# Attention on transposed scores without the row maximum, behind a test of the gains, with TensorE in program order

## The chip, the cores and the metric

The kernel runs on one core of a Trainium2 chip. The metric is the device time of one execution in microseconds (us), lower is better. A core has five engines that run beside each other and wait for each other by semaphores: TensorE (PE: products and transposes; PEld: its weight loads), VectorE (DVE), ScalarE (ACT), GpSimd (POOL) and SyncE (SP, which issues the DMAs here). [...]

## The reference

Everything is fp32, but the weights w_in and w_out arrive as doubles and are rounded in the kernel. Cut to what matters:

```python
batch, n_heads, seq, head_dim = (8, 12, 448, 64)
q_n, k_n = (rmsnorm(q, g_q), rmsnorm(k, g_k))
scores = q_n @ k_n.T / sqrt(64)
attn = exp(scores - max(scores, axis=-1))
attn = attn / (sum(attn, axis=-1) + 1e-09)
x = (attn @ v)                      # to (3584, 768)
h = maximum(x @ w_in, 0)            # w_in 768 x 2048
out = (h * h) @ w_out               # w_out 2048 x 768
```

rmsnorm divides a row of 64 by its root mean square and multiplies it by the gains g.

## The kernel before

Attention runs on one pair of heads at a time: 2 x 64 makes 128 partitions, 6 pairs in a batch, 48 in all. The 448 tokens of a sequence are split as token = 4 p + j, with p on 112 partitions.

For a pair i, `load` brings q, k and v (SP). `norm` makes the normalised rows qkn on POOL (squares, a sum on DVE, a power, two products with the factors). `transposes` turns them in eight PE transposes into the PSUM tile pt, and DVE writes them with the gains as qkT, with the head's 64 elements on the partitions.

A unit of work is one j of the queries of one pair, four a pair. `softmax(i, j)` makes the scores sc of 112 queries by 448 keys, for the two heads; DVE takes the maximum of each row (nmax), ACT makes the exponentials pr and their sums, DVE the reciprocal and the scaling of pr. `values(i, j)` transposes pr with eight PE transposes (ppt), copies them out (prT; ACT and DVE one head each), and multiplies them with v into pav, four products a head. After the fourth unit pav goes to xT, which is x transposed.

`feed_forward(b)` is a generator: 16 pieces of the first product ph (six products of 448 columns, then ACT's relu, then POOL's square into gT), then pieces of the second product po (of 384 columns; 16 accumulate one half of 128 tokens; six such halves in an even batch, eight in an odd one). The main loop lays the feed-forward pieces of batch b - 1 between the units of batch b; batch 0 has none, and in it the weights are loaded and rounded instead (`round_weights`: DVE, ACT and POOL, 32 pieces). The feed-forward block of batch 7 runs alone at the end.

The order on each engine is decided by the framework's scheduler, from its own estimate of when an instruction could start; the program's order is its starting point. Tiles come from pools with a number of buffers (`bufs`), and a buffer's next use waits until its readers are done. [...]

Of the kernel before, what the change touches and what calls it, by code (L numbers as in the profile page):

```python
# [1 line left out]

# [6 lines left out]
F32 = mybir.dt.float32  # L9
U32 = mybir.dt.uint32  # L10
AF = mybir.ActivationFunctionType
ALU = mybir.AluOpType
AX = mybir.AxisListType.X


@with_exitstack
def kernel(
    ctx: ExitStack,
    tc: tile.TileContext,
    q: bass.AP,  # L20
# [5 lines left out]
    w_out: bass.AP,  # L26
    out: bass.AP,
):
    """Softmax attention with RMS-normalised q and k, then relu(x w_in)^2 w_out, all in fp32.

    Attention runs on one pair of heads at a time (2 x 64 = 128 partitions).
    A sequence of 448 tokens is split as token = 4 p + j, with p on 112
    partitions, so that a partition's 4 tokens are one run in memory. A unit of
    work is one j of the queries of one pair: scores and softmax with the
    queries on the partitions, then the normalised rows are transposed and
    multiplied with v, which gives x transposed, as the first product of the
    feed-forward block takes it. The feed-forward block of a batch is laid
    between the units of the next batch.
    """
    nc = tc.nc  # L40

    B, H, S, D = q.shape
    NT, DM = out.shape
    DFF = w_in.shape[1]
    P = 128
    NJ = 4
    SP = S // NJ
    NPAIR = H // 2
    NFC = DFF // P
    HALF = DM // 2  # L50
    REST = S % P
    FULL = S - REST
# [3 lines left out]
    consts = ctx.enter_context(tc.tile_pool(name="consts", bufs=1))  # L56
    loads = ctx.enter_context(tc.tile_pool(name="loads", bufs=2))
    work = ctx.enter_context(tc.tile_pool(name="work", bufs=2))
    small = ctx.enter_context(tc.tile_pool(name="small", bufs=4))
    ps_s = ctx.enter_context(tc.tile_pool(name="ps_s", bufs=2, space=bass.MemoryType.PSUM))  # L60
    ps_o = ctx.enter_context(tc.tile_pool(name="ps_o", bufs=1, space=bass.MemoryType.PSUM))
    ps_m = ctx.enter_context(tc.tile_pool(name="ps_m", bufs=3, space=bass.MemoryType.PSUM))

    ident = consts.tile([P, P], F32, name="ident")
    gains = consts.tile([P, 2], F32, name="gains")
    mhalf = consts.tile([SP, 2 * 2 * NJ], F32, name="mhalf")
    w1 = consts.tile([P, NPAIR, DFF], F32, name="w1")
    w2 = consts.tile([P, NFC, DM], F32, name="w2")
    gT = consts.tile([P, NFC, S + REST], F32, name="gT")
    rebias = consts.tile([P, 1], F32, name="rebias")  # L70

# [1 line left out]
    # Doubles come in pairs of words (low, high) and are rounded here to fp32, the  # L73
    # widest type of the engines: +-2^E from the high word, times
    # 1 + (m20 + low 2^-32) 2^-20. Below fp32's normal range a weight becomes 0,
    # above it infinite. The words stay in gT until the feed-forward block needs it.
    NW = 768
    NSET = 3
    spare = gT.rearrange("p f n -> p (f n)")
    assert NSET * 3 * NW <= NFC * (S + REST)  # L80
    doubles = w_in.dtype != F32
    words_in = 2 if doubles else 1
    w1r, w2r = ((w.bitcast(U32) if doubles else w).rearrange("(c p) n -> p c n", p=P) for w in (w_in, w_out))
    CW = NPAIR // 2
    FW = NW // CW
    pieces_w = [(w1[:, c:c + CW, f:f + FW], w1r[:, c:c + CW, words_in * f:words_in * (f + FW)])
                for f in range(0, DFF, FW) for c in (0, CW)]
# [28 lines left out]
        nc.vector.scalar_tensor_tensor(wu, high, 0x80000000, wu, ALU.bitwise_and, ALU.bitwise_or)  # L116
        nc.gpsimd.tensor_tensor(w, f, w, ALU.mult)  # L117

# [1 line left out]
    qks, vs, qkTs, probs, pavs, xTs = {}, {}, {}, {}, {}, {}  # L120

    def load(i):
        b, h0 = i // NPAIR, 2 * (i % NPAIR)
        qk = loads.tile([SP, 2, 2, NJ * D], F32, tag="qk", name="qk")
        vt = loads.tile([SP, 2, NJ, D], F32, tag="vt", name="vt", bufs=3)
        for dst, src in ((qk[:, 0], q), (qk[:, 1], k), (vt.rearrange("p h j d -> p h (j d)"), v)):
            nc.sync.dma_start(dst, src[b, h0:h0 + 2].rearrange("h (p j) d -> p h (j d)", j=NJ))
        qks[i], vs[i] = qk, vt

    normed = {}  # L130
# [20 lines left out]
    def transposes(i):  # L151
        qkn = normed.pop(i)
        qkT = work.tile([P, 2, S], F32, tag="qkT", name="qkT")
        for s in range(2):
            pt = ps_m.tile([P, S], F32, tag="m", name="pt")
            for j in range(NJ):
                nc.tensor.transpose(pt[:, j * SP:(j + 1) * SP],
                                    qkn[:, s, j].rearrange("p h d -> p (h d)"), ident[:SP, :SP])
            nc.vector.tensor_scalar(qkT[:, s], pt, gains[:, s:s + 1], None, ALU.mult)  # L159
        qkTs[i] = qkT  # L160
# [49 lines left out]
                                  pav.rearrange("d (j p) -> d j p", j=NJ))  # L210
            del pavs[i], vs[i]

# [1 line left out]
    # gT has room for 448 + 64 tokens. An even batch takes the last 448 columns  # L214
    # and leaves its last 64 tokens there for the odd batch that follows, which
    # takes the first 448 and shares its last block of 128 with them.
    def feed_forward(b):
        xT = xTs.pop(b)
        odd = b % 2
        c0 = 0 if odd else REST  # L220
        for f in range(NFC):
            ph = ps_m.tile([P, S], F32, tag="m", name="ph")
            for c in range(NPAIR):
                nc.tensor.matmul(ph, w1[:, c, f * P:(f + 1) * P], xT[:, c, :],  # L224
                                 start=(c == 0), stop=(c == NPAIR - 1))
            r = work.tile([P, S], F32, tag="r", name="r")
            nc.scalar.activation(r, ph, AF.Relu)  # L227
            nc.gpsimd.tensor_tensor(gT[:, f, c0:c0 + S], r, r, ALU.mult)  # L228
            yield
        for t in range(0, FULL + P * odd, P):  # L230
            osb = work.tile([P, DM], F32, tag="osb", name="osb")
            for half in range(2):
                cols = slice(half * HALF, (half + 1) * HALF)
                po = ps_m.tile([P, HALF], F32, tag="m", name="po")
                for f in range(NFC):
                    nc.tensor.matmul(po, gT[:, f, c0 + t:c0 + t + P], w2[:, f, cols],  # L236
                                     start=(f == 0), stop=(f == NFC - 1))
                    if f == NFC // 2 - 1:
                        yield
                if half == 0:  # L240
                    nc.vector.tensor_copy(osb[:, cols], po)  # L241
                else:
                    nc.scalar.copy(osb[:, cols], po)
                if half == 1:
                    if t < FULL:
                        nc.sync.dma_start(out[b * S + t:b * S + t + P, :], osb)
                    else:
                        nc.sync.dma_start(out[b * S + FULL:(b + 1) * S, :], osb[0:REST])
                        nc.sync.dma_start(out[(b - 1) * S + FULL:b * S, :], osb[REST:P])
                yield  # L250

    def pieces(b):
        return NFC + 4 * (FULL // P + b % 2)

# [1 line left out]
    load(0)  # L256
    for i, g in enumerate((g_q, g_k)):
        for h in range(2):
# [11 lines left out]
    NP = B * NPAIR  # L270
    last = None
    for b in range(B):
        fill = feed_forward(b - 1) if b else iter(())  # starts at its first next()
        n = pieces(b - 1) if b else 0
        done = 0
        for u in range(NPAIR * NJ):
            i, j = b * NPAIR + u // NJ, u % NJ
            if j == 0 and i + 2 < NP:
                load(i + 2)
            softmax(i, j)  # L280
            if j == 1 and i + 1 < NP:
                norm(i + 1)
            if j == 3 and i + 1 < NP:
                transposes(i + 1)
            if last is not None:
                values(*last)
            last = (i, j)
            if b == 0:
                m = len(pieces_w)
                for n_w in range(m * u // (NPAIR * NJ), m * (u + 1) // (NPAIR * NJ)):  # L290
                    round_weights(n_w)
                    load_weights(n_w + NSET)
            while done < n * (u + 1) // (NPAIR * NJ):
                next(fill)
                done += 1
        for _ in fill:
            pass
# [2 lines left out]
        pass  # L300


# [1 line left out]
_INS = ['q', 'k', 'v', 'g_q', 'g_k', 'moe_w_in', 'moe_w_out']  # L304
_OUTS = [((3584, 768), 'float32')]
# [25 lines left out]
```

## Time and profile before

| | us |
|---|---|
| median of three runs | 2096.86 (2093.71 to 2096.97) |
| the profiled execution | 2093.7 |
| its span, first to last instruction | 2093.7 |
| PE busy | 1981.1 |
| DVE busy | 838.1 |
| POOL busy | 535.5 |
| ACT busy | 494.4 |

PE's busy time counts the records of products, which overlap and whose ends are modelled: the distance between starts tells more of what a product costs. [...] Names such as ph<-xT,w say which tile is written from which; L224 is line 224 of the kernel before.

### The profile page before, as it was taken

Reading aid. Unit: us, or ns where it says so; the run is one execution under the profiler, and the core shown is the slowest. Engines: PE = TensorE matmul, PEld = TensorE weight load, DVE = VectorE, ACT = ScalarE, POOL = GpSimd, SP = SyncE. Lnnn points to the kernel's source line nnn. Section 1 sums busy time; section 2 is a strip of 40 time slices with the busy share of each in tenths; the row PEclk is TensorE's granted clock in tenths of the full one; section 3 lists DMA queues with packets and bytes.
Section 4 is the critical chain, followed back from the end, with each engine's and each line's share of the span. In section 5 each row is a group of like instructions: output and inputs, shape, how many; then the busy total and the mean of one; then the engine's idle time right before and its main releaser. Section 6 shows DMA issues by size and latency. Waiting matters only on the chain.

```text
span 2093.7 us, 22618 instructions
## 1 busy us (share of the span) xinstructions
PE 1981.1 (95%) x9088; PEld 1130.0 (54%) x9088; DVE 838.1 (40%) x1533; ACT 494.4 (24%) x1181; POOL 535.5 (26%) x408
## 2 busy tenths in 40 slices
PE   4767699999999999999999999999999999999999
PEld 2444455555555555555555555555555555555555
DVE  7898853333333333333333333333333333333000
ACT  2344332212221222212221122212222122221100
POOL 4345542311321132311231123221231113210100
PEclk7566599999999999999999999999999999999999
DMA  4233300000000010010000000001000000000000
GB/s 149 93 128 104 123 27 13 28 29 21 23 18 21 29 31 17 14 35 29 14 23 26 29 21 27 14 21 42 14 14 33 31 21 15 17 8 16 0 8 23
DMA packets 47784, 70.67 MB, mean 34 GB/s; under 512 B 3648, under 2 KB 35904, under 8 KB 47680
## 3 DMA queue, kind: packets, MB, share of 16 engines
q1 hardware_dynamic: 47680, 69.22, 10.2%
q8 instruction: 73, 1.20, 0.2%
q14 instruction: 31, 0.25, 0.0%
HBM read 58.20 MB, written 11.01 MB: 33 GB/s over the span
## 4 chain that ended last, share of the span: by engine, by line
PE 81%; DVE 13%; issue 5%; POOL 1%; DMA 0%; SPq 0%; ACT 0%; POOLq 0%; DVEq 0%; ACTq 0%
PE ph L224 29%; PE po L236 25%; PE pav L204 12%; PE sc L167 8%; PE ppt L195 7%; DVE nmax L170 3%; DVE pr L180 1%; DVE qkT L159 1%; DVE w L116 1%; DVE gT L113 1%; DVE gT L112 1%; DVE w L110 1%; DVE rstd L140 1%; DVE w L115 1%; POOL qkn L137 1%
## 5 line engine op out<-in xcount | busy, mean ns | idle before, releaser
L224 PE MATMUL ph<-xT,w 128*128 128x448 f32 x1536 | 626.8, 549 | 1.1 <-DVE xT L209 1.1
L236 PE MATMUL po<-w,gT 128*128 128x384 f32 x1792 | 617.7, 492 | 0.0
L170 DVE TENSOR_REDUCE nmax<-sc 112x2 f32<-112x896 f32 x192 | 209.2, 1090 | 799.2 <-PE sc L167 799.2
L236 PEld LDWEIGHTS po<-w,gT 128*128 128x128 f32 x1792 | 326.7, 190 | 207.8 <-DVE qkT L159 2.8
L224 PEld LDWEIGHTS ph<-xT,w 128*128 128x128 f32 x1536 | 275.0, 190 | 231.2 <-issue 208.0
L204 PEld LDWEIGHTS pav<-prT,vt 112*64 112x64 f32 x3072 | 275.2, 144 | 165.4 <-ACT prT L198 104.3
L204 PE MATMUL pav<-prT,vt 112*64 112x112 f32 x3072 | 334.4, 278 | 6.8 <-DVE prT L200 6.2
L228 POOL TENSOR_TENSOR gT<-r 128x448 f32<-128x448 f32 x128 | 119.4, 933 | 752.7 <-ACT r L227 752.7
L174 ACT ACTIVATE pr<-sc,nmax 112x448 f32<-112x448 f32 x384 | 240.2, 630 | 184.8 <-DVE nmax L170 180.3
L167 PE MATMUL sc<-qkT 64*112 64x448 f32 x768 | 228.9, 626 | 34.0 <-DVE qkT L159 17.5
L195 PE MATMUL ppt<-ident,pr 112*112 112x112 f32 x1536 | 207.8, 277 | 42.6 <-DVE pr L180 23.1
L195 PEld LDWEIGHTS ppt<-ident,pr 112*112 112x112 f32 x1536 | 158.4, 140 | 152.9 <-issue 113.4
L137 POOL TENSOR_TENSOR qkn<-qk 112x1024 f32<-112x1024 f32 x48 | 91.8, 1912 | 533.3 <-issue 380.7
L227 ACT ACTIVATE r<-ph 128x448 f32<-128x448 f32 x128 | 69.6, 544 | 602.5 <-PE ph L224 602.5
L198 ACT COPY prT<-ppt 112x448 f32<-112x448 f32 x192 | 102.1, 532 | 412.6 <-PE ppt L195 412.6
L180 DVE TENSOR_SCALAR pr<-pr,rec 112x448 f32<-112x448 f32 x384 | 174.5, 497 | 5.8
L142 POOL TENSOR_TENSOR rstd<-rstd,mhalf 112x16 f32<-112x16 f32 x48 | 139.6, 2909 | 4.0
L167 PEld LDWEIGHTS sc<-qkT 64*112 64x112 f32 x768 | 61.1, 183 | 147.3 <-issue 105.2
L200 DVE COPY prT<-ppt 112x448 f32<-112x448 f32 x192 | 118.0, 614 | 16.0 <-PE ppt L195 15.9
L144 POOL TENSOR_TENSOR qkn<-qk,rstd 112x512 f32<-112x512 f32 x96 | 107.1, 1136 | 3.8
L241 DVE COPY osb<-po 128x384 f32<-128x384 f32 x28 | 15.6, 558 | 229.0 <-PE po L236 229.0
L117 POOL TENSOR_TENSOR w<-gT,w 128x768 f32<-128x768 f32 x32 | 65.4, 2047 | 112.5 <-DVE w L116 65.3
(27 smaller groups left out, 630.4 us busy)
## 6 DMA issues: line engine op xcount, KB each, us to landing
gT<-in_moe_w_in_dram SPq DMA_DIRECT2D x16, 768.0 KB, 4.5
gT<-in_moe_w_out_dram SPq DMA_DIRECT2D x16, 768.0 KB, 4.2
qk<-in_q_dram SPq DMA_DIRECT2D x48, 224.0 KB, 2.7
qk<-in_k_dram SPq DMA_DIRECT2D x48, 224.0 KB, 2.9
vt<-in_v_dram SPq DMA_DIRECT2D x48, 224.0 KB, 2.5
out_dram<-osb SPq DMA_DIRECT2D x24, 384.0 KB, 2.3
out_dram<-osb SPq DMA_DIRECT2D x8, 192.0 KB, 2.6
gains<-in_g_q_dram SPq DMA_DIRECT2D x2, 0.2 KB, 2.8
```

The costliest lines, as they stand in the source:

```text
L137: nc.gpsimd.tensor_tensor(sq, flat, flat, ALU.mult)
L142: nc.gpsimd.tensor_tensor(rflat, rflat, mhalf, ALU.pow)
L167: nc.tensor.matmul(sc[:, h, 0:S], qkT[rows, 0, j * SP:(j + 1) * SP], qkT[rows, 1, :], start=True, stop=True)
L170: nc.vector.tensor_reduce(nmax, sc[:, :, 0:S], AX, ALU.max, negate=True)
L174: nc.scalar.activation(pr[:, h], sc[:, h, 0:S], AF.Exp, bias=nmax[:, h:h + 1], accum_out=total[:, h:h + 1])
L180: nc.vector.tensor_scalar(pr[:, h], pr[:, h], rec[:, h:h + 1], None, ALU.mult)
L195: nc.tensor.transpose(pt[:, c, :], pr[:, h, c * SP:(c + 1) * SP], ident[:SP, :SP])
L200: nc.vector.tensor_copy(prT, pt)
L204: nc.tensor.matmul(pav[h * D:(h + 1) * D, j * SP:(j + 1) * SP], vt[:, h, c, :], prTs[h][:, c, :], start=(c == 0), stop=(c == NJ - 1))
L224: nc.tensor.matmul(ph, w1[:, c, f * P:(f + 1) * P], xT[:, c, :], start=(c == 0), stop=(c == NPAIR - 1))
L228: nc.gpsimd.tensor_tensor(gT[:, f, c0:c0 + S], r, r, ALU.mult)
L236: nc.tensor.matmul(po, gT[:, f, c0 + t:c0 + t + P], w2[:, f, cols], start=(f == 0), stop=(f == NFC - 1))
```

## The change

The function above stays, as `attention_then_ffn_with_row_max`. Beside it stands a second one, `attention_then_ffn_bounded`, and the kernel chooses between them at run time: it loads the two gains, takes the largest (g_q g_k)^2, and every engine loads that number into a register and branches. If it is at most 75^2 / 64 = 87.9, no score can exceed 75, the exponentials don't need the row maximum, and the bounded function runs. With the reference's gains the number is 27.7.

In the bounded function the scores are made transposed, with the keys on the partitions: `scores(i, c)` has 112 keys by 448 queries for the two heads, and one ACT operation makes the exponentials pr of both. pr is then already the operand that `values` needs, so its transposes and copies are gone; a product is 448 columns wide instead of 112, and the two heads alternate. POOL adds the four pr of a pair into acc, and `finish(i)` multiplies acc with a tile of ones, which gives the sums of the columns (tot) on 64 partitions; DVE takes the reciprocal of 128 x 448 and multiplies pav with it. The loads of v are issued apart from those of q and k. A block of work is now two key chunks, twelve blocks a batch, and feed-forward pieces of po are whole halves. `ps_m` has two buffers, `ps_o` a second tile (tot). The relu writes into gT and POOL squares it there.

The bounded function runs under `manual_schedule` for PE: PE's instructions keep the order in which the program is written. The other engines are still ordered by the scheduler.

```diff
-def tile_qk_norm_attention__then__act_relu_squared_kernel(
+def attention_then_ffn_with_row_max(
...
+    ps_m = ctx.enter_context(tc.tile_pool(name="ps_m", bufs=2, space=bass.MemoryType.PSUM))
...
+    def scores(i, c):
+
+        qkT = qkTs[i]
+        sc = ps_s.tile([SP, 2, 512], F32, tag="s", name="sc")
+        for h in range(2):
+            rows = slice(h * D, (h + 1) * D)
+            nc.tensor.matmul(sc[:, h, 0:S], qkT[rows, 1, c * SP:(c + 1) * SP], qkT[rows, 0, :],
+                             start=True, stop=True)
+        pr = work.tile([SP, 2, S], F32, tag="pr", name="pr", bufs=5)
+        nc.scalar.activation(pr, sc[:, :, 0:S], AF.Exp)
+        probs[i, c] = pr
+        if c == 1:
+            accs[i] = work.tile([SP, 2, S], F32, tag="acc", name="acc")
+            nc.gpsimd.tensor_tensor(accs[i], probs[i, 0], pr, ALU.add)
+        elif c > 1:
+            nc.gpsimd.tensor_tensor(accs[i], accs[i], pr, ALU.add)
+        if c == NJ - 1:
+            del qkTs[i]
+
+    def values(i, cs):
+        if 0 in cs:
+            pavs[i] = ps_o.tile([P, S], F32, tag="o", name="pav")
+        for c in cs:
+            pr = probs.pop((i, c))
+            for h in range(2):
+                nc.tensor.matmul(pavs[i][h * D:(h + 1) * D, :], vs[i][:, h, c, :], pr[:, h, :],
+                                 start=(c == 0), stop=(c == NJ - 1))
+
+    def finish(i):
+        b, hp = divmod(i, NPAIR)
+        acc = accs.pop(i)
+        tot = ps_o.tile([P, S], F32, tag="t", name="tot")
+        for h in range(2):
+            nc.tensor.matmul(tot[h * D:(h + 1) * D, :], ones, acc[:, h, :], start=True, stop=True)
+        rec = work.tile([P, S], F32, tag="rec", name="rec", bufs=1)
+        nc.vector.reciprocal(rec, tot)
...
+        nc.vector.tensor_tensor(xTs[b][:, hp, :].rearrange("d (p j) -> d j p", j=NJ),
+                                pavs.pop(i).rearrange("d (j p) -> d j p", j=NJ),
+                                rec.rearrange("d (j p) -> d j p", j=NJ), ALU.mult)
+        del vs[i]
...
+            if not second:
+                if i + 2 < NP:
+                    load(i + 2)
+                scores(i, 0)
+                scores(i, 1)
+                if i + 1 < NP:
+                    norm(i + 1)
+                if u:
+                    values(i - 1, (2, 3))
+                    finish(i - 1)
+            else:
+                if i + 1 < NP:
+                    load_v(i + 1)
+                    transposes(i + 1)
+                scores(i, 2)
+                scores(i, 3)
+                values(i, (0, 1))
...
+            if u == blocks - 1:
+                values(i, (2, 3))
+                finish(i)
+            while done < n * (u + 1) // blocks:
+                next(fill)
+                done += 1
...
+    for i, g in enumerate((g_q, g_k)):
+        nc.sync.dma_start(gg[:, i, :], g.rearrange("(o d) -> o d", o=1))
+    nc.vector.tensor_tensor(gg[:, 0, :], gg[:, 0, :], gg[:, 1, :], ALU.mult)
+    nc.vector.tensor_tensor(gg[:, 0, :], gg[:, 0, :], gg[:, 0, :], ALU.mult)
+    nc.vector.tensor_reduce(top, gg[:, 0, :], AX, ALU.max)
+
+    bits = nc.values_load(top.bitcast(mybir.dt.int32))
+    limit = struct.unpack("<i", struct.pack("<f", 75.0 ** 2 / D))[0]
+    args = (q, k, v, g_q, g_k, w_in, w_out, out)
+    with tc.If(bits <= limit) as small_scores:
+        with tc.manual_schedule(engines={mybir.EngineType.PE}):
+            attention_then_ffn_bounded(tc, *args)
+    with small_scores.Else():
+        attention_then_ffn_with_row_max(tc, *args)
```

What this makes of PE's order, in a stretch of a batch that has ph pieces between. Before, a unit and a half (L167 the scores, L195 the transposes of pr, L204 the values, L224 the feed-forward; L157 transposes q and k of the next pair):

```order
L224 MATMUL ph<-xT,w_79 128x448 x5
L167 MATMUL sc<-qkT 112x448 x2
L157 MATMUL pt<-ident,qkn 128x112 x8
L195 MATMUL ppt<-ident,pr 112x112 x8
L224 MATMUL ph<-xT,w_79 128x448
L204 MATMUL pav<-prT,vt 64x112 x4
L224 MATMUL ph<-xT,w_79 128x448
L204 MATMUL pav<-prT,vt 64x112 x4
L224 MATMUL ph<-xT,w_79 128x448 x4
L167 MATMUL sc<-qkT 112x448 x2
```

Now, a whole pair of heads (two blocks) and the end of the one before, where the line numbers are those of the changed file (L465 scores, L484 values, L492 the column sums, L513 ph, L454 the transposes of q and k):

```order
L492 MATMUL tot<-acc,ones 64x448 x2
L513 MATMUL ph<-xT,w_100 128x448 x12
L454 MATMUL pt<-ident,qkn 128x112 x8
L465 MATMUL sc<-qkT 112x448 x4
L484 MATMUL pav<-pr,vt 64x448 x4
L513 MATMUL ph<-xT,w_100 128x448 x12
L465 MATMUL sc<-qkT 112x448 x4
L484 MATMUL pav<-pr,vt 64x448 x4
L492 MATMUL tot<-acc,ones 64x448 x2
```

Between the transposes pt and the column sums tot, twelve products of ph stand in this order. In the last block of a batch they don't (L525 is po):

```order
L525 MATMUL po<-w_101,gT 128x384 x32
L454 MATMUL pt<-ident,qkn 128x112 x8
L465 MATMUL sc<-qkT 112x448 x4
L484 MATMUL pav<-pr,vt 64x448 x8
L492 MATMUL tot<-acc,ones 64x448 x2
L525 MATMUL po<-w_101,gT 128x384 x32
```

There tot follows the values at once, and the po pieces come behind it. POOL's order at that place, with the numbers of the tiles: qkn_1488 is the norm of the pair after next (its first row waits for pt of the pair before it), acc_1335 the sum that the tot above reads.

```order
L472 TENSOR_TENSOR acc_1335<-pr_1328,pr_1333 112x896
L434 TENSOR_TENSOR qkn_1488<-qk_1322 112x1024
L438 TENSOR_SCALAR rstd_1490<-rstd_1490 112x16
L439 TENSOR_TENSOR rstd_1490<-rstd_1490,mhalf_99 112x16
L441 TENSOR_TENSOR qkn_1488<-qk_1322,rstd_1490 112x2x4x64
L474 TENSOR_TENSOR acc_1335<-acc_1335,pr_1411 112x896
L441 TENSOR_TENSOR qkn_1488<-qk_1322,rstd_1490 112x2x4x64
L474 TENSOR_TENSOR acc_1335<-acc_1335,pr_1417 112x896
```

The norm's first four rows stand ahead of both last additions to acc, its fifth between them. From batch 1 on the same rows stand in this order in every pair of heads.

## Rows read from the trace of the kernel before

**Rows 1.** The page: PE's busy time, and the chain by engine.

```profile
PE 1981.1 (95%) x9088; PEld 1130.0 (54%) x9088; DVE 838.1 (40%) x1533; ACT 494.4 (24%) x1181; POOL 535.5 (26%) x408
...
PE 81%; DVE 13%; issue 5%; POOL 1%; DMA 0%; SPq 0%; ACT 0%; POOLq 0%; DVEq 0%; ACTq 0%
```

**Rows 2.** Busy us by stage: length, PE, PEld, DVE, ACT, POOL; clock, DMA share, GB/s.

```profile
0.00:265.00 265.00, 177.05 (x716) 110.11 (x717) 225.47 (x324) 97.65 (x182) 124.78 (x74) 0.64 0.36 118
265.00:1935.00 1670.00, 1650.28 (x7929) 935.53 (x7928) 609.79 (x1206) 386.12 (x980) 395.76 (x318) 1.00 0.07 23
1935.00:2093.70 158.70, 153.80 (x446) 84.36 (x444) 2.86 (x5) 10.62 (x20) 14.91 (x16) 1.00 0.03 10
```

**Rows 3.** PE's order in time, mid-run: start, length, operation, count, wait.

```profile
1021.68 1.01 PE L167 MATMUL sc<-qkT 64*112 64x448 f32 x4
1022.62 0.98 PE L195 MATMUL ppt<-ident,pr 112*112 112x112 f32 x8
1023.44 0.93 PE L224 MATMUL ph<-xT,w 128*128 128x448 f32 x2
1024.30 1.42 PE L204 MATMUL pav<-prT,vt 112*64 112x112 f32 x16
1025.65 8.54 PE L224 MATMUL ph<-xT,w 128*128 128x448 f32 x22
1034.12 1.01 PE L167 MATMUL sc<-qkT 64*112 64x448 f32 x4
...
1044.83 0.59 PE L195 MATMUL ppt<-ident,pr 112*112 112x112 f32 x4 [0.49 <-DVE qkT L159]
```

**Rows 4.** The same view, a stretch with the second product.

```profile
1182.23 9.94 PE L236 MATMUL po<-w,gT 128*128 128x384 f32 x30
1192.10 1.01 PE L167 MATMUL sc<-qkT 64*112 64x448 f32 x4
```

**Rows 5.** Groups by line, POOL and DVE: busy us, mean ns, idle before.

```profile
L142 POOL TENSOR_TENSOR rstd<-rstd,mhalf 112x16 f32<-112x16 f32 x48 | 139.6, 2909 | 4.0
L228 POOL TENSOR_TENSOR gT<-r 128x448 f32<-128x448 f32 x128 | 119.4, 933 | 752.7 <-ACT r L227 752.7
...
L144 POOL TENSOR_TENSOR qkn<-qk,rstd 112x512 f32<-112x512 f32 x96 | 107.1, 1136 | 3.8
...
L137 POOL TENSOR_TENSOR qkn<-qk 112x1024 f32<-112x1024 f32 x48 | 91.8, 1912 | 533.3 <-issue 380.7 <-PE pt L157 141.5 <-DVE rec L178 3.3
...
L140 DVE TENSOR_REDUCE rstd<-qkn 112x16 f32<-112x1024 f32 x48 | 58.5, 1218 | 27.0 <-POOL qkn L137 27.0
```

**Rows 6.** End of batch 0: PE's order, and two stretches as in rows 2.

```profile
257.61 0.96 PE L195 MATMUL ppt<-ident,pr 112*112 112x112 f32 x4 [3.99 <-DVE pr L180]
...
235.00:262.00 27.00, 15.27 (x78) 10.88 (x77) 27.00 (x40) 11.97 (x23) 17.76 (x9) 0.64 0.38 131
262.00:300.00 38.00, 36.37 (x178) 19.95 (x178) 23.69 (x42) 12.15 (x27) 19.45 (x14) 0.99 0.06 19
```

**Rows 7.** Two small operations of DVE: shortest, median and longest in ns.

```profile
L177 DVE TENSOR_SCALAR total<-total x192: 146/165/1852, 23.3 to 1921.4; 112x2 f32<-112x2 f32 x192
...
L178 DVE RECIPROCAL rec<-total x192: 148/166/167, 23.8 to 1921.6; 112x2 f32<-112x2 f32 x192
```

**Rows 8.** Groups by line, DVE: busy us, mean ns, idle before.

```profile
L170 DVE TENSOR_REDUCE nmax<-sc 112x2 f32<-112x896 f32 x192 | 209.2, 1090 | 799.2 <-PE sc L167 799.2
...
L180 DVE TENSOR_SCALAR pr<-pr,rec 112x448 f32<-112x448 f32 x384 | 174.5, 497 | 5.8
...
L200 DVE COPY prT<-ppt 112x448 f32<-112x448 f32 x192 | 118.0, 614 | 16.0 <-PE ppt L195 15.9
...
L209 DVE COPY xT<-pav 128x448 f32<-128x448 f32 x48 | 46.0, 959 | 73.3 <-PE pav L204 73.3
```

**Rows 9.** The start: a load of gains (KB, us to landing), PE's first work.

```profile
gains<-in_g_q_dram SPq DMA_DIRECT2D x2, 0.2 KB, 2.8
...
12.03 2.01 PE L157 MATMUL pt<-ident,qkn 112*128 112x112 f32 x8 [12.03 <-POOL qkn L144]
```

More of the change, by code (lines that the diff above doesn't have):

```diff
@@ L1 @@
+import struct
 from contextlib import ExitStack
@@ L16 @@
 @with_exitstack
-def kernel(
+def attention_then_ffn_with_row_max(
     ctx: ExitStack,
@@ new lines, with kernel @@
+@with_exitstack
+def kernel(
+    ctx: ExitStack,
+    tc: tile.TileContext,
+    q: bass.AP,
+    k: bass.AP,
+    v: bass.AP,
+    g_q: bass.AP,
+    g_k: bass.AP,
+    w_in: bass.AP,
+    w_out: bass.AP,
+    out: bass.AP,
+):
+    nc = tc.nc
+    D = q.shape[-1]
+    bound = ctx.enter_context(tc.tile_pool(name="bound", bufs=1))
+    gg = bound.tile([1, 2, D], F32, name="gg")
+    top = bound.tile([1, 1], F32, name="top")
+    for i, g in enumerate((g_q, g_k)):
+        nc.sync.dma_start(gg[:, i, :], g.rearrange("(o d) -> o d", o=1))
[10 more added lines that the diff above has]
+        attention_then_ffn_with_row_max(tc, *args)
```

187 lines of the change are left out of this document (added).

## The prediction

> **What bounds the kernel now.** I read the page first, then the busy time by stages, then PE's order in time. PE is busy for 95% of the span, and the chain that ended last is PE for 81% [rows 1], so PE's own work is the thing to cost. The stages differ, though [rows 2]. Batch 0 (to 265 us, where the first feed-forward product starts) has no feed-forward work to fill PE: DVE is busy for 225.5 of 265 us there, PE has waits and a mean granted clock of 0.64. From 265 to 1935 us PE is busy for 1650 of 1670 us at clock 1.00: seven batches of attention, with the feed-forward block of the batch before laid between. The last 158.7 us are the feed-forward block of batch 7 alone.
>
> In the middle stage I price PE by the distance between starts, since the ends are modelled [rows 3]. An fp32 product is two records (passes). Twenty-two passes of ph take 1034.12 - 1025.65 = 8.47 us, 0.385 us each with the change of shape at both ends; thirty passes of po take 9.87 us, 0.329 each [rows 4]. The stage holds 7 x 16 x 6 = 672 products of ph (1344 passes) and 4 x 96 + 3 x 128 = 768 of po (1536 passes): 517.4 + 505.3 = 1022.7 us, which the change leaves alone. What is left, 1670 - 1022.7 = 647 us over 42 pairs of heads, is 15.4 us a pair of attention: four units, each sc 0.94, ppt 0.82, pav 1.35 [rows 3], and pt 0.82 once, make 13.3; the rest is heads that are split by other products and waits.
>
> **Scores transposed.** The probabilities come out with keys on the partitions, so the 32 transposes ppt per pair, their copies, the row maximum and the scaling go. In sc the two heads work on different rows of the array and run side by side: two products, four passes, in 0.94 us, where one after the other would be 4 x 0.385 = 1.54. So a side-by-side pair is 2 x 0.385 + 0.17 for the change of shape. In the new order two sc pairs stand together: 4 x 0.385 + 0.17 = 1.71, twice a pair of heads, 3.42.
>
> pav has as many columns as before (4 x 2 products of 448 instead of 32 of 112), but the two heads now alternate. Today each head's four products stand together, and still 16 passes take 1.35 us, where 16 at ppt's pace of 0.102 would be 1.64: the heads, on different columns of the array, overlap in part. Alternating, I take them as fully side by side, like sc: 1.71 for (0, 1); for (2, 3) with the added column sums tot behind them, 6 x 0.385 + 0.17 = 2.48. The other end, no overlap, is a rival. With pt 0.82 a pair of heads costs 3.42 + 1.71 + 2.48 + 0.82 = 8.43, over 42 pairs 354 us.
>
> **PE in program order: where it waits.** Three places.
>
> First, pt with two ps_m buffers instead of three: its second half needs the buffer of the product just ended, emptied by ACT. A wait of that kind is 0.49 us today (PE for DVE's qkT, [rows 3]); 0.45 x 42 = 19 us.
>
> Second, tot needs the sum acc, which POOL makes. On POOL the whole norm of the pair after next stands before the last two additions (the order of POOL shown with the change), and it starts when pt is done. POOL's chain from there [rows 5]: 1.91 for the squares, 1.22 on DVE, 2.91 for the power, two products of 1.14, and two additions over 896 columns. No addition of that size is in the trace; by 933 ns for 448 it is 1.87, by 1912 for 1024 it is 1.67; I take 1.87. That is 12.1, with 0.7 for one small operation and the handovers 12.8 us, and 0.3 more until the last transpose has landed: 13.1. PE meanwhile, counted from the end of pt: sc 1.71, pav 1.71, two pieces of feed-forward (24 passes, 9.2), sc 1.71, pav 1.6: 15.9. So tot finds its sum ready with 2.8 us to spare, in every block but the last of a batch. There finish stands before the feed-forward pieces: sc 1.71 and pav 8 x 0.385 = 3.1 make 4.8, and PE waits 13.1 - 4.8 = 8.3 us (7.9 at the other price of the addition, 12 with additions twice as slow; nothing, if norm came behind them, which the order excludes). Queued behind tot are the po pieces, with nothing of their own to wait for. Six batches (1 to 6) have it in this stage: 50 us; batch 7 has no norm left, 1 us.
>
> Third, after such a wait the clock. Batch 0's waits of 4 us go with 0.64 between 235 and 262 us; after the one before 257.61 us PE runs on, and 262 to 300 has 0.99 already [rows 6]. So full clock was back within some 5 us, which at half pace loses 2.5: six times, 15 us (0 if the clock holds; 60 if all 21 us of po ran at half).
>
> The reciprocal of 128 x 448 and the product behind it keep pav's only buffer until the next pair's values. The trace has a reciprocal of 112 x 2 alone: 166 ns, against 165 for an addition of that size [rows 7]. Two elements can hide at most about 20 ns, 10 per element, so 448 cost between the 0.61 us of a copy of that width [rows 8] and 5 us; I take 3. From tot to the next pav PE has 9.2 + 0.82 + 1.71 = 11.7 us of other work, which covers 3 + 0.96. [...]
>
> **Batch 0.** DVE's share is 0.85 [rows 2]. Each of its 24 units loses nmax 1.09, two pr of 0.50, one prT of 0.61, and the two small ones of 0.165: 3.03 us [rows 7, 8], 72.7 in all; xT's copy of 0.96 becomes a product of the same size; six reciprocals add 18. 225.5 - 72.7 + 18 = 170.8, at 0.85 it is 201 us. In DVE's queue the reciprocal waits for tot with weight rounding behind it; PE at half clock needs about 16 us from pt to tot (8.43 doubled, less the first sc), DVE has some 12 of work between: 4 us x 6 = 24 if none of it is in the 0.85 already, 0 if all is; I take 7.
>
> The new start comes ahead: the gains are loaded (2.8 us for such a load [rows 9], 0.5 for the second), three small DVE operations make 0.5, then each engine loads a register and branches, for which the trace has no row: between 0 and the 12 us that PE waits for its first work today [rows 9]; I take 3, one more fetch like the load. 7 us, and nothing hides it. [...] Batch 0: 201 + 7 + 7 = 215 (195 to 245), 50 less than now.
>
> **The sum** against the profiled execution's 2093.7: 215 + 1022.7 + 354 + 19 + 50 + 1 + 15 + 159 for the last stage (unchanged: with two buffers, one is still emptied while the next product fills the other) = 1836. The median shown, 2096.86, lies 3 above that execution; so 1839.
>
> **Rivals.**
> *The sum is late in every block*: if POOL's additions are slow, or its norm queues behind feed-forward squares, by more than the 2.8 us to spare. Additions twice as slow (3.7 us more) would do it; 3 us beyond the point cost 3 x 36 = 108: 1947. Against it: POOL is busy for 396 of 1670 us [rows 2] and gets 42 x 3 x 1.87 = 236 more, so it is free for over half of the time.
> *pav and tot don't overlap*: five pairs of products a pair of heads, 0.77 more each, 48 times: 185, 2024. Against it: the 1.35 above.
> *Fewer waits*: the last block's wait and the clock's loss don't come, batch 0 ends at 195: 1839 - 65 - 20 = 1754.
> *Slower, by the reciprocal*: pav's buffer comes free R + 1.2 after tot, and PE has 11.7 us of cover. The gain is 260 us, 5.4 a pair; from R = 16 on it is gone, at R = 20 the 42 pairs lose 9.5 each, batch 0 another 100: 2340. For it, only that no row has the size; against it the equal 166 and 165 ns.
> *The change doesn't do what it says*: the gains exceed the bound, and the row-maximum branch runs: 2097 + 7 = 2104. The largest squared product of gains from the reference's seed is 27.7, the limit 87.9.
>
> **How the numbers follow.** The forecast, 1839 with its own range 1780 to 1905 (batch 0's bounds, and the clock's), has 0.74; the late sum 0.10, no overlap 0.05, fewer waits 0.05, the reciprocal 0.03, the other branch 0.03. From 1770 to 1930 lie nearly all of the forecast and about half of its two neighbours. A measurement here tells 0.2% from no change (the three runs spread over 0.16%). Faster: 0.94; slower 0.05; the same 0.01, from the other branch with a short start.
>
> **What would show it.** After: first ph near 215 us and DVE's share there still near 0.85; sc, pav and tot with the two heads starting nearly together; PE idle before tot some 8 us in one block of each batch, released by POOL, and none in the others; the clock below 1.00 behind each; a reciprocal of about 3 us, with no PE wait on DVE's product. The forecast is wrong if PE waits before tot or pav in every block, if one head's passes start only when the other's end, or if batch 0 doesn't end by 245.

## The result, and the profile after

| | us |
|---|---|
| before, median of four runs | 2095.81 (2093.71 to 2096.97) |
| after, median of four runs | 1853.1 (1851.87 to 1854.97) |
| ratio, with its 95% interval | 0.8845 (0.8832 to 0.8857) |
| forecast | 1839, range 1770 to 1930 |

The kernel is 11.6% faster; 243 us were gained, 258 forecast. The page of the kernel after, beside [rows 1], with the granted clock of 40 slices of the span (PEclk, the share of full speed that TensorE was given, in tenths):

```profile
PE 1624.2 (88%) x5440; PEld 804.5 (43%) x5440; DVE 496.7 (27%) x432; ACT 304.4 (16%) x413; POOL 833.4 (45%) x553
...
PEclk9657679998999999999999999999999999999999
...
PE 81%; POOL 4%; DVE 2%; ACT 1%; issue 0%; POOLq 0%; ACTq 0%
```

PE has 357 us less of busy time, but its share fell from 95 to 88%, and POOL, 1% of the chain before, is now 4%. Busy time by stage, to be read against [rows 2] (start:end, length, PE, PEld, DVE, ACT, POOL, clock, DMA share, GB/s; the first feed-forward product starts at 230.8, the block of batch 7 at 1689.4):

```profile
0.00:230.80 230.80, 83.23 (x281) 31.94 (x281) 196.99 (x184) 72.83 (x85) 163.54 (x92) 0.70 0.43 135
230.80:1689.40 1458.60, 1386.16 (x4714) 687.65 (x4714) 297.50 (x245) 220.41 (x308) 654.93 (x445) 0.98 0.08 25
1689.40:1850.50 161.10, 154.85 (x449) 84.90 (x447) 2.23 (x4) 11.11 (x21) 14.91 (x16) 0.99 0.04 13
```

Batch 0 is 34 us shorter than its 265, the middle stage 211 shorter than its 1670; the last stage is 2 longer. The middle stage's granted clock is 0.98 where it was 1.00. PE's order in time, one pair of heads and the start of the next, beside [rows 3]:

```profile
701.91 1.72 PE L484 MATMUL pav<-pr,vt 112*64 112x448 f32 x8
703.56 9.29 PE L513 MATMUL ph<-xT,w 128*128 128x448 f32 x24
712.78 1.76 PE L465 MATMUL sc<-qkT 64*112 64x448 f32 x8
714.47 1.72 PE L484 MATMUL pav<-pr,vt 112*64 112x448 f32 x8
716.02 0.92 PE L492 MATMUL tot<-acc,ones 112*64 112x448 f32 x4
716.88 9.29 PE L513 MATMUL ph<-xT,w 128*128 128x448 f32 x24
726.00 0.55 PE L454 MATMUL pt<-ident,qkn 112*128 112x112 f32 x4
726.80 0.60 PE L454 MATMUL pt<-ident,qkn 112*128 112x112 f32 x4 [0.25 <-ACT gT L516]
727.33 1.76 PE L465 MATMUL sc<-qkT 64*112 64x448 f32 x8
```

The distances between starts give the prices: sc 714.47 - 712.78 = 1.69 (1.71 forecast), pav of the first two chunks 703.56 - 701.91 = 1.65 (1.71), pav with tot 716.88 - 714.47 = 2.41 (2.48). From pt to sc it is 1.33; pt alone was priced at 0.82, so its wait costs 0.51 (0.45 forecast), of which the trace shows 0.25 as idle time. No wait stands before tot here. In the last block of a batch one does. All engines there, batch 2:

```profile
629.09 1.89 POOL L434 TENSOR_TENSOR qkn<-qk 112x1024 f32<-112x1024 f32 x1 [21.36 <-PE pt L454]
...
630.57 3.23 PE L484 MATMUL pav<-pr,vt 112*64 112x448 f32 x16
...
639.62 2.07 POOL L474 TENSOR_TENSOR acc<-acc,pr 112x896 f32<-112x896 f32 x1
...
641.75 1.76 PE L492 MATMUL tot<-acc,ones 112*64 112x448 f32 x4 [7.95 <-POOL acc L474]
...
643.56 2.96 DVE L494 RECIPROCAL rec<-tot 128x448 f32<-128x448 f32 x1 [11.32 <-PE tot L492]
```

PE is done with pav and sits for 7.95 us until POOL, which began the norm at 629.09, ends its last addition at 641.69. tot then runs slowly (1.76 us where it took 0.92 above): the granted clock, 1.00 up to the end of pav, is 0.50 behind the wait (columns as in the stages):

```profile
627.57:633.75 6.18, 5.95 (x33) 2.42 (x31) 2.59 (x3) 2.21 (x3) 3.23 (x3) 1.00 0.16 64
641.75:645.00 3.25, 3.25 (x7) 1.25 (x8) 1.44 (x1) 0.00 (x0) 0.00 (x0) 0.50 0.45 127
```

The kernel before has the same level behind its wait at the end of batch 0, the half pace of the forecast:

```profile
257.60:261.60 4.00, 3.31 (x16) 2.65 (x16) 4.00 (x8) 0.53 (x1) 1.64 (x1) 0.50 0.01 4
```

The two stretches of the changed kernel behind the first of its waits (that tot starts at 422.1):

```profile
422.00:428.00 6.00, 5.93 (x12) 2.73 (x13) 3.91 (x2) 0.00 (x0) 0.01 (x1) 0.55 0.25 68
428.00:440.00 12.00, 12.00 (x39) 7.10 (x38) 0.56 (x1) 0.00 (x0) 0.00 (x0) 1.00 0.00 0
```

At a mean of 0.55 for 6 us, 2.7 us are lost; 2.5 was the forecast. In the six us behind the other five waits the clock is 0.50 to 0.73, and all six together lose 13 us; 15 was the forecast.

### The profile page after: what moved, and what is told of

The parts are those of the page before. It is cut to its first block, busy times and chain, and to the rows that moved or that the text cites. A ratio compares the mean times of both kernels' runs of the same rounds, so it can differ in the third digit from the quotient of the medians.

```text
span 1850.5 us, 13250 instructions
## 1 busy us (share of the span) xinstructions
PE 1624.2 (88%) x5440; PEld 804.5 (43%) x5440; DVE 496.7 (27%) x432; ACT 304.4 (16%) x413; POOL 833.4 (45%) x553
## 4 chain that ended last, share of the span: by engine, by line
PE 81%; POOL 4%; DVE 2%; ACT 1%; issue 0%; POOLq 0%; ACTq 0%
PE po L525 32%; PE ph L513 32%; PE sc L465 7%; PE pav L484 6%; PE tot L492 2%; POOL acc L474 2%; PE pt L454 1%; POOL rstd L439 1%; ACT gT L516 1%; POOL qkn L441 1%; POOL qkn L434 1%; DVE rstd L437 0%; DVE w L407 0%; ACT osb L530 0%; DVE w L408 0%
## 5 line engine op out<-in xcount | busy, mean ns | idle before, releaser
L513 PE MATMUL ph<-xT,w 128*128 128x448 f32 x1536 | 595.6, 544 | 7.6 <-DVE xT L497 7.6
L525 PE MATMUL po<-w,gT 128*128 128x384 f32 x1792 | 592.3, 492 | 0.0
L525 PEld LDWEIGHTS po<-w,gT 128*128 128x128 f32 x1792 | 342.5, 192 | 256.0 <-issue 27.5
L513 PEld LDWEIGHTS ph<-xT,w 128*128 128x128 f32 x1536 | 287.5, 190 | 314.1 <-issue 305.6
L494 DVE RECIPROCAL rec<-tot 128x448 f32<-128x448 f32 x48 | 141.9, 2956 | 554.5 <-PE tot L492 554.5
L517 POOL TENSOR_TENSOR gT<-gT 128x448 f32<-128x448 f32 x128 | 118.3, 933 | 293.9 <-ACT gT L516 293.9
L465 PE MATMUL sc<-qkT 64*112 64x448 f32 x768 | 188.5, 614 | 60.1 <-DVE qkT L456 60.1
L472 POOL TENSOR_TENSOR acc<-pr 112x896 f32<-112x896 f32 x48 | 102.8, 2141 | 287.3 <-ACT pr L468 287.1
L474 POOL TENSOR_TENSOR acc<-acc,pr 112x896 f32<-112x896 f32 x96 | 201.1, 2095 | 27.5 <-ACT pr L468 27.1
L468 ACT ACTIVATE pr<-sc 112x896 f32<-112x896 f32 x192 | 166.9, 913 | 157.5 <-PE sc L465 157.5
L516 ACT ACTIVATE gT<-ph 128x448 f32<-128x448 f32 x128 | 69.7, 544 | 596.4 <-PE ph L513 596.4
L484 PE MATMUL pav<-pr,vt 112*64 112x448 f32 x768 | 167.4, 561 | 0.0
L456 DVE TENSOR_SCALAR qkT<-pt,gains 128x448 f32<-128x448 f32 x96 | 65.3, 682 | 340.0 <-PE pt L454 338.9
L454 PE MATMUL pt<-ident,qkn 112*128 112x112 f32 x384 | 62.1, 289 | 98.0 <-POOL qkn L441 88.5
L465 PEld LDWEIGHTS sc<-qkT 64*112 64x112 f32 x768 | 67.1, 189 | 141.8 <-issue 133.5
L528 DVE COPY osb<-po 128x384 f32<-128x384 f32 x28 | 15.6, 558 | 349.2 <-PE po L525 349.2
L454 PEld LDWEIGHTS pt<-ident,qkn 112*128 112x128 f32 x384 | 45.3, 153 | 132.2 <-POOL qkn L441 83.0
L484 PEld LDWEIGHTS pav<-pr,vt 112*64 112x64 f32 x768 | 48.3, 139 | 115.1 <-issue 90.2
```

The costliest lines, as they stand in the source:

```text
L454: nc.tensor.transpose(pt[:, j * SP:(j + 1) * SP], qkn[:, s, j].rearrange("p h d -> p (h d)"), ident[:SP, :SP])
L465: nc.tensor.matmul(sc[:, h, 0:S], qkT[rows, 1, c * SP:(c + 1) * SP], qkT[rows, 0, :], start=True, stop=True)
L468: nc.scalar.activation(pr, sc[:, :, 0:S], AF.Exp)
L474: nc.gpsimd.tensor_tensor(accs[i], accs[i], pr, ALU.add)
L484: nc.tensor.matmul(pavs[i][h * D:(h + 1) * D, :], vs[i][:, h, c, :], pr[:, h, :], start=(c == 0), stop=(c == NJ - 1))
L494: nc.vector.reciprocal(rec, tot)
```

## The experiments

There are ten kernels, each measured against the kernel before on the same chip. Where an edit is to the changed kernel, its time is to be set against 1853.1. That time is of another set of runs; the kernel before took 2095.3 to 2095.8 us beside all of them, so the sets agree within 0.03%.

**No test.** The bounded function is called directly:

```diff
-    bits = nc.values_load(top.bitcast(mybir.dt.int32))
...
-    with tc.If(bits <= limit) as small_scores:
-        with tc.manual_schedule(engines={mybir.EngineType.PE}):
-            attention_then_ffn_bounded(tc, *args)
+    with tc.manual_schedule(engines={mybir.EngineType.PE}):
+        attention_then_ffn_bounded(tc, *args)
```

> The bounded function is called directly: no load of the gains' maximum, no register, no branch. Theory: the test costs what it delays the first load of q, 4.05 against 0.73 us in the two traces, and nothing hides it: 1853.1 - 3.3 = 1850. Rival: batch 0 is bound by VectorE and GpSimd from 15 us on and takes the delay up: 1853. [...]

Measured: 1850.18 (1849.47 to 1853.33), ratio 0.8836 (0.8824 to 0.8848). That is 2.9 us less, as the first theory had it. But the two ranges overlap, so it is likely, not settled, that nothing hides the delay. The trace shows the first load of q at 0.72 us again.

**The other branch.** `75.0 ** 2 / D` becomes `0.0 ** 2 / D`, and the row-maximum function runs behind the test.

> The limit is set to zero, so the kernel takes its second branch: the row-maximum function as before, behind the test. Theory: 3.3 us of delay at the start and nothing else, 2095.8 + 3.3 = 2099. Rival: the jump past the bounded function's code is dear on every engine, 5 to 10 us more: 2104 to 2110. If the delay is hidden in batch 0: 2096.

Measured: 2103.05 (2099.91 to 2103.59), ratio 1.0035 (1.0021 to 1.0049): 7.6 us more than the 2095.41 beside it, between the two forecasts. Its start (order in time, SP's and DVE's rows; `top` is ready at 3.14):

```profile
2.93 0.21 DVE L629 TENSOR_REDUCE top<-gg 1x1 f32<-1x64 f32 x1
7.16 0.34 SPq L128 DMA_DIRECT2D qk<-in_q_dram  x1
```

and the same two rows of the changed kernel, which goes on into the bounded function:

```profile
3.19 0.21 DVE L629 TENSOR_REDUCE top<-gg 1x1 f32<-1x64 f32 x1
...
4.05 0.34 SPq L418 DMA_DIRECT2D qk<-in_q_dram  x1
```

From the number to the first load it takes 0.65 us into the code that follows, 4.0 into the code behind the bounded function: the jump costs 3.4 us more. The trace shows what moves meanwhile: between 3.2 and 7.2 us the only transfers are five packets of the two instruction queues, 0.05 MB. The changed kernel has no such packet between 3.4 and 15 us. Against the kernel before, whose first load starts at 0.73, the delay is 6.4 of the 7.6 us.

**PE ordered by the scheduler.** The line `with tc.manual_schedule(...)` is left out.

> The bounded function with TensorE's order left to the scheduler. Theory: the gain comes from the transposed scores, and the order is nearly the same without the instruction to keep it (the first score product moves between the two halves of pt, where 0.25 us of wait stood 42 times): 1843 to 1860. Rival: the kept order is a large part of the gain, and without it waits come back in every pair of heads: above 1880.

Measured: 1871.98 (1867.93 to 1875.01), ratio 0.8929 (0.8915 to 0.8943). 19 us slower: more than the theory's range, less than the rival's. In PE's order in time the scheduler has put one score product between the halves of pt:

```profile
758.33 0.55 PE L454 MATMUL pt<-ident,qkn 112*128 112x112 f32 x4
758.81 1.00 PE L465 MATMUL sc<-qkT 64*112 64x448 f32 x2
759.75 0.61 PE L454 MATMUL pt<-ident,qkn 112*128 112x112 f32 x4
760.28 1.75 PE L465 MATMUL sc<-qkT 64*112 64x448 f32 x6
761.97 1.73 PE L484 MATMUL pav<-pr,vt 112*64 112x448 f32 x8
```

That fills the wait, but splits a pair: one head's two passes take 759.75 - 758.81 = 0.94 alone, the time in which two heads run side by side, and the other head runs alone in the x6. From pt to pav it is 3.64 us, in program order 1.33 + 1.69 = 3.02 (rows above). So it goes in 40 of the 42 pairs, which makes 0.62 x 40 = 25 us, and the middle stage is 1486.5 - 1458.6 = 28 longer. Its batch 0 is 5 us shorter.

**Heads apart.** In the values, one head's products before the other's:

```diff
-        for c in cs:
-            pr = probs.pop((i, c))
-            for h in range(2):
+        prs = {c: probs.pop((i, c)) for c in cs}
+        for h in range(2):
+            for c in cs:
+                pr = prs[c]
```

> In the values, the two products of one head stand together before those of the other, instead of alternating. Theory: TensorE starts a head's products as soon as the other head's are all handed on, and with 4 passes a head that is almost at once: under 0.2 us a block, 1853 to 1872. Rival, as the prediction priced it: the heads overlap only because they alternate; without it 4 pairs of products a pair of heads cost 0.75 us more each, 48 times: 1997.

Measured: 1853.84 (1852.24 to 1856.83), ratio 0.8846 (0.8833 to 0.886): no change. From sc to pav to tot, in its order in time:

```profile
717.92 1.73 PE L485 MATMUL pav<-pr,vt 112*64 112x448 f32 x8
719.48 0.93 PE L493 MATMUL tot<-acc,ones 112*64 112x448 f32 x4
```

Eight passes in 1.56 us, as with alternating heads (716.02 - 714.47 = 1.55). One after the other, eight passes would take 8 x 0.385 = 3.1. The records of this pav start in twos, 14 ns apart (717.92, 717.94, 718.35, 718.36 and so on), and the two that report a head as done are the last two. So the heads do run side by side, as forecast, but not because they alternate: in these records the second head's passes start beside the first head's, behind which they stand in the program.

**The row maximum, in program order.** The kernel before with `manual_schedule` around it, the second half of the change alone.

> The kernel before, row maximum and transposes of the probabilities as they were, with TensorE alone kept in program order: the second half of the change by itself. Theory: the order is no source of the gain; the units' chains are covered by the unit between as before, and what changes is small waits: 2075 to 2135. Rival: the order brings a good part of the 243 us: below 2040.

Measured: 2200.1 (2193.39 to 2211.45), ratio 1.0489 (1.046 to 1.0517). It is slower than either forecast: the order alone costs 105 us. The group of the values:

```profile
L204 PE MATMUL pav<-prT,vt 112*64 112x112 f32 x3072 | 340.9, 277 | 150.8 <-DVE prT L200 89.7 <-ACT prT L198 60.3
```

In the order as written, the values follow their transposes at once and wait for the copies: 150.8 us of idle PE stand before them, 6.8 in the kernel before, whose scheduler puts a product of ph between (1023.44 in [rows 3]). Not all of it is lost in the time: the first product of ph starts at 250.1 us here, 15 earlier than in the kernel before. The transposed scores took away just the step that needed such filling.

**The last sums on PE.** In the last pair of heads of batches 1 to 7, POOL adds two of the four chunks, PE sums the rest into tot:

```diff
+        by_pool = 2 if i % NPAIR == NPAIR - 1 and i >= NPAIR else NJ
+        sums.setdefault(i, [])
+        if c >= by_pool:
+            sums[i].append(pr)
-        if c == 1:
+        elif c == 1:
             accs[i] = work.tile([SP, 2, S], F32, tag="acc", name="acc")
             nc.gpsimd.tensor_tensor(accs[i], probs[i, 0], pr, ALU.add)
+            sums[i].append(accs[i])
...
+        for n, part in enumerate(parts):
+            for h in range(2):
+                nc.tensor.matmul(tot[h * D:(h + 1) * D, :], ones, part[:, h, :],
+                                 start=(n == 0), stop=(n == len(parts) - 1))
```

> For the last pair of heads of batches 1 to 7, GpSimd adds only the first two key chunks, long before, and TensorE sums the other two itself: three products a head into tot instead of one. Theory: the wait of 7.95 us before tot goes six times (48), the clock no longer falls (13 lost behind the six waits), two more pairs of products come seven times (2 x 0.75 x 7 = 10.5): 1853 - 50 = 1803, with no clock below 1.00 between 260 and 1840 us. Rival: something else is late at that place (the reciprocal, the next norm), and the wait moves: above 1840.

Measured: 1800.87 (1800.12 to 1801.3), ratio 0.8593 (0.8579 to 0.8608). That is 52 us less; 50 was forecast. No wait stands before tot from batch 1 on, and over this stretch the granted clock is full (columns as in the stages):

```profile
260.00:1796.00 1536.00, 1522.83 (x5179) 766.42 (x5178) 282.74 (x231) 224.10 (x319) 621.30 (x436) 1.00 0.08 25
```

**Batch 0's sums on PE.** The same code with `by_pool = 0 if i < NPAIR else NJ`.

> In batch 0 alone TensorE sums all four key chunks (four products a head into tot), and GpSimd adds nothing. Theory: GpSimd's additions hold up VectorE's rounding of the weights (5.8 us of VectorE a piece now, 4.2 before) and delay the norm that TensorE waits for; without them the rounding falls to about 4.5 us a piece and the first feed-forward product comes 25 to 40 us earlier: 1815 to 1830. Rival: the rounding is longer because less else stands between, not for the additions: 5.5 us or more a piece, and 1845 to 1860. The added products cost 3 x 0.75 x 6 = 14 us of TensorE at full clock, 27 at half, where it is idle over half of the time.

Measured: 1821.96 (1820.03 to 1825.55), ratio 0.8699 (0.8684 to 0.8713). That is 31 us less, and the first ph starts at 199.6 instead of 230.8. DVE is busy for 170.3 of these 199.6 us, the same share of 0.85. DVE's groups for the rounding up to 230.8 us (busy us, mean ns, idle before), first of the changed kernel:

```profile
L407 DVE TENSOR_SCALAR w<-w 128x768 uint32<-128x768 uint32 x29 | 40.0, 1378 | 19.8 <-ACT w L403 19.8
L405 DVE SCALAR_TENSOR_TENSOR gT<-gT 128x768 f32<-128x768 uint32 x30 | 39.2, 1307 | 0.0
L408 DVE SCALAR_TENSOR_TENSOR w<-gT,w 128x768 uint32<-128x768 uint32 x29 | 36.5, 1257 | 0.0
L404 DVE TENSOR_SCALAR gT<-gT 128x768 uint32<-128x768 uint32 x30 | 28.9, 963 | 0.0
L402 DVE TENSOR_SCALAR w<-gT 128x768 uint32<-128x768 uint32 x31 | 28.2, 911 | 4.4 <-DMA gT<-in_moe_w_in_dram 4.4
```

then of this one:

```profile
L405 DVE SCALAR_TENSOR_TENSOR gT<-gT 128x768 f32<-128x768 uint32 x32 | 36.7, 1146 | 0.0
L408 DVE SCALAR_TENSOR_TENSOR w<-gT,w 128x768 uint32<-128x768 uint32 x32 | 35.0, 1095 | 0.0
L407 DVE TENSOR_SCALAR w<-w 128x768 uint32<-128x768 uint32 x32 | 31.0, 968 | 15.4 <-ACT w L403 15.4
L402 DVE TENSOR_SCALAR w<-gT 128x768 uint32<-128x768 uint32 x32 | 28.4, 889 | 4.3 <-DMA gT<-in_moe_w_in_dram 4.3
L404 DVE TENSOR_SCALAR gT<-gT 128x768 uint32<-128x768 uint32 x32 | 23.8, 743 | 0.0
```

and of the kernel before, up to 265 us, with two groups that the change removes:

```profile
L180 DVE TENSOR_SCALAR pr<-pr,rec 112x448 f32<-112x448 f32 x48 | 37.4, 820 | 0.0
L113 DVE SCALAR_TENSOR_TENSOR gT<-gT 128x768 f32<-128x768 uint32 x31 | 32.6, 1052 | 0.0
L116 DVE SCALAR_TENSOR_TENSOR w<-gT,w 128x768 uint32<-128x768 uint32 x30 | 32.0, 1065 | 0.0
...
L110 DVE TENSOR_SCALAR w<-gT 128x768 uint32<-128x768 uint32 x32 | 24.4, 762 | 5.9 <-DMA gT<-in_moe_w_in_dram 5.9
L112 DVE TENSOR_SCALAR gT<-gT 128x768 uint32<-128x768 uint32 x31 | 22.7, 731 | 0.0
L115 DVE TENSOR_SCALAR w<-w 128x768 uint32<-128x768 uint32 x30 | 18.6, 619 | 0.0
L177 DVE TENSOR_SCALAR total<-total 112x2 f32<-112x2 f32 x24 | 15.1, 627 | 0.5 <-ACT pr L174 0.5
```

The five means of a piece make 4.23 us before, 5.82 after and 4.84 with no additions on POOL. So taking POOL's additions away shortens DVE's work by 0.98 us a piece, 31 us over 32 pieces, as much as the time saved (in part by another way: POOL itself is freer for the norm). The other 0.61 us of the rise stays without them. Where it comes from can be read in single records. One operation's shortest, median and longest time in batch 0, the kernel before and the changed one:

```profile
L115 DVE TENSOR_SCALAR w<-w x30: 544/670/692, 17.9 to 257.7; 128x768 uint32<-128x768 uint32 x30
L407 DVE TENSOR_SCALAR w<-w x29: 541/683/2568, 20.7 to 223.1; 128x768 uint32<-128x768 uint32 x29
```

The median is the same; some are far longer. Two of these, with what POOL does beside them, in the changed kernel:

```profile
101.40 4.25 POOL L474 TENSOR_TENSOR acc<-acc,pr 112x896 f32<-112x896 f32 x2 [0.84 <-ACT pr L468]
...
104.40 1.79 DVE L407 TENSOR_SCALAR w<-w 128x768 uint32<-128x768 uint32 x1 [3.03 <-ACT w L403]
...
109.02 2.39 POOL L409 TENSOR_TENSOR w<-gT,w 128x768 f32<-128x768 f32 x1 [1.43 <-DVE w L408]
109.67 2.29 DVE L407 TENSOR_SCALAR w<-w 128x768 uint32<-128x768 uint32 x1
```

Each begins while POOL is at work and ends 0.54 and 0.55 us after POOL's operation, and 0.54 is the shortest time that it takes by itself: by these records it is held until POOL is done. The first stands beside the additions, the second beside POOL's own product of the rounding, which the change leaves alone. I set every record of batch 0 against the mean of those with nothing on POOL beside them. In the changed kernel the five operations take 59 us too long, by the POOL operation that each overlaps most: 27 beside that product, 19 beside the additions, 13 beside the norm. With no additions it is 33, of which 25 beside the product. In the kernel before it is 13, but the two operations that the change removes (pr and the small one) take another 30 too long, and 31 of these 43 us stand beside the product. So the holding by POOL's product was there before the change; it passed from the removed operations to the rounding, and that is the 0.61.

**All sums on DVE.** `nc.gpsimd.tensor_tensor(accs[i], ...)` becomes `nc.vector.tensor_tensor`.

> All additions of the exponentials on VectorE instead of GpSimd. Theory: the wait before the last tot of a batch goes with its clock loss (61 us), as with the sums on TensorE, and batch 0 loses little, since VectorE's 18 additions (about 1 us each) come against rounding that is no longer held up: 1785 to 1805. Rival: batch 0 is bound by VectorE's work and grows by 20 to 35 us: 1812 to 1830.

Measured: 1792.63 (1792.16 to 1793.62), ratio 0.8556 (0.8541 to 0.857). That is 60 us less. The middle stage is 1400.2 us long, and no wait before tot in it is longer than 0.8 us. Batch 0 ends at 228.8, 2 us earlier. The rounding is shorter there by 1.03 us a piece (4.79), but DVE has the 18 additions, 1.76 us each for 12 of them and 1.35 for the other six where about 1 was expected, 29 us in all; and before the last tot of batch 0 PE waits 15.6 us for DVE's addition.

**Two edits together.** PE sums four chunks in batch 0 and two in the last pair of the later batches.

> The two edits together: TensorE sums all four key chunks in batch 0, and two of four in the last pair of later batches; GpSimd keeps the other additions. Theory: the two savings are of different stages and add: 1853.1 - 52.2 - 31.1 = 1770. Rival: the end of batch 0 and the start of batch 1 share a bound, and part of one saving is lost: 1778 to 1790.

Measured: 1768.41 (1767.69 to 1773.61), ratio 0.8447 (0.8432 to 0.8461). The savings add: 84.7 us were saved, and the two alone give 52.2 + 31.1 = 83.3.

**Batch 0 on PE, the rest on DVE.**

> Batch 0's sums on TensorE, all later additions on VectorE, none on GpSimd. Theory: batch 0 as in the run with its sums on TensorE (first feed-forward product near 199 us) and the later stage as in the run with all sums on VectorE (1400 us): 1792.6 - 29 = 1763. Rival: VectorE's additions come later than GpSimd's in some blocks and take the difference back: 1770 or more.

Measured: 1769.45 (1766.67 to 1771.65), ratio 0.8444 (0.843 to 0.8458): the same as the one before within its spread, 6 us over the theory and at the rival's edge. Its first ph starts at 203.5 us, 4 later than with batch 0's edit alone; PE waits 3.3 us longer there for DVE's qkT, and why it does stays open. These two are the fastest kernels of the study.

## Why the prediction was right

**PE's sum.** The middle stage was forecast at 1022.7 + 354 + 19 + 50 + 1 + 15 = 1462 us and took 1458.6. The mechanism held: twelve products of ph took 712.78 - 703.56 = 9.22 us (24 x 0.385 = 9.24 forecast), and the prices of products side by side came out within 0.1 us a block. That the sum is only 3 us off is in part luck, as told below under the two waits. The premise that alternating makes the heads run side by side failed on its reason: heads apart run so too (1.56 us against 1.55). The rival of no overlap fell with it.

**The wait in the last block.** It took 7.95 us, six times, released by POOL's addition; 8.3 was forecast, from POOL's order and five rows of the trace before. An addition took 2.07, not 1.87, and a product with the factors 1.04, not 1.14. No row stood beside the 0.7 for the small operation and the handovers and the 0.3 until the last transpose has landed: here the first is 0.36 (12.60 from 629.09 to 641.69, less 12.24 for the operations priced), and POOL begins 0.21 us after the transposes are handed on. Taking the wait away gave the wait and the clock's loss back, as the sum had them. From batch 1 on tot waited in no other block, but for 1.55 us at the end of batch 7 (1 in the sum), so the late-sum rival fell as well. In batch 0 it waited twice, 4.61 and 0.54 us.

**The reciprocal.** It took 2.96 us, 3 in the sum, and PE waits for the product behind it only once, at the end of batch 0.

**The start.** The first load comes 3.3 us later instead of 7: the branch into the bounded function is 0.65 us from number to load, where the sum took 3 for a register and a branch; no run shows these 3. In the other branch the same stretch is 4.0 us, 3.4 longer, and packets of the instruction queues stand in it.

**Batch 0 was mis-sized**: 215 forecast, 230.8 measured, as much as the 14 us by which the forecast is off (the other two stages, 3 less and 2 more, nearly cancel). The share of DVE came out as assumed (196.99 of 230.8 is 0.85). The step that failed is "225.5 - 72.7 + 18 = 170.8": DVE's work is 197. It priced the removed operations by their means and medians over the whole run, and the rounding as unchanged. In batch 0 two of the removed ones were dearer (pr 0.820 against 0.497, the small one 0.627 against a median of 0.165): of the 30 us that they took too long, 23 stand beside POOL's product. With them gone, that holding falls on the rounding, and POOL's additions hold it too: 1.59 us a piece in all. Even so the miss is smaller than the step: 197 at the share of 0.85 is 232 us by itself, which leaves no room for the 7 us of the start and the 7 of DVE's queue that the forecast adds. The start was 3.3 us, and no row shows the queue's term apart.

**Two waits at the start of batch 1** were not in the sum. PE's order in time there:

```profile
243.37 1.86 PE L513 MATMUL ph<-xT,w 128*128 128x448 f32 x2 [7.56 <-DVE xT L497]
251.40 2.01 PE L454 MATMUL pt<-ident,qkn 112*128 112x112 f32 x8 [6.16 <-POOL qkn L441]
```

They make 13.7 us. The middle stage came out right although it holds them, because others of its terms were too high: a pair of heads without its waits took 8.26 us instead of 8.43 (7 us over 42 pairs), and 32 products of po in one run took 20.75 (387.19 to 407.94) where 64 x 0.329 = 21.1 was forecast (some 7 us over 24 of them). That these cancel is luck. The small waits and the clock came out within 2 us each.

**The parts of the change.** The bounded function with its transposed scores, under the scheduler's order, takes 1872, 223 us less than before. Program order on top of it gives 19 us, and program order on the old scores costs 105. So the gain is the bounded function's; the order is worth something only behind it. What its own parts are worth (no row maximum, no transposes of pr, wider products) was not measured apart.

## What to carry to other kernels

Where one engine is the bound, the distance between starts of its operations prices a change of its work, here within a few per cent. The order of the helping engines tells where the new waits come: look for the block in which the usual cover is missing, here the last of a batch. A helper that another holds up must be priced together with it, in the stage where both are busy and with that stage's own means: here, taking operations away from the one did not remove the holding (43 us of batch 0 before, 59 after), which passed to the operations that were left. In the two cases here, keeping the written order paid where no operation needs its neighbour's result at once (19 us), and cost time where one does (105 us).

## What the runs showed of the hardware

Eight passes of pav, four a head, take 1.56 us with one head's written ahead of the other's and 1.55 with the heads alternating; at the 0.385 us of a pass of ph, one after the other, they would take 3.1. With the heads apart their records start in twos, 14 ns apart.

The five VectorE operations of the rounding, and in the kernel before the scaling of pr and the small operation, were held in batch 0 by GpSimd's operations, 59 us in the changed kernel and 43 in the kernel before, also by additions on tiles that they neither read nor write: two that begin beside an addition and beside a product on GpSimd end 0.54 and 0.55 us after it, and the same operation takes 0.54 at its shortest. Not every operation was held: the row maximum of the kernel before took 1.07 to 1.10 us in all of batch 0, beside GpSimd's product or not.
